# An attention and gated-MLP kernel: the second layer as seven half-size products, the first on 384 tokens at a time

## The chip, the cores and the metric

The kernel runs on one core of a Trainium2 chip. The metric is the time of one execution on the device, in microseconds (us). Three executions of the kernel before took 736.87, 735.04 and 735.07 us, a median of 735.07. One further execution was profiled; it took 735.57 us, of which its trace covers a span of 733.3 us. The core has five engines that work side by side: TensorE (PE in the profile; its weight loads are PEld) multiplies matrices into PSUM, VectorE (DVE) and ScalarE (ACT) work element by element, GpSimd (POOL) helps, and SP's queue issues nearly all transfers between the chip's memory and SBUF.

## The reference

Inputs are q, k, v of 4 batches x 8 heads x 768 positions x 64, and weights w_in (512 x 2,048) and w_out (2,048 x 512), the weights in float64.

```python
scores = scale * np.matmul(q, k.transpose(0, 1, 3, 2))
is_global = pos[None, :] < int(n_global)                 # n_global = 8
is_local = (rel >= 0) & (rel < int(n_local))             # n_local = 96
bias = -slopes[:, None, None] * dist[None, :, :]
scores = np.where(is_global | is_local, scores + bias, -1000000000.0)
a = softmax(scores)
x = (a @ v) as 3072 tokens x 512
h = x @ w_in
g = h * (1.0 / (1.0 + np.exp(-h)))
out = g @ w_out                                          # 3072 x 512, float32
```

Each position looks at 8 global positions and at the 96 up to itself. The two products of the MLP are 3,072 x 512 x 2,048 and 3,072 x 2,048 x 512.

## The kernel before, in words

The 3,072 tokens are 24 blocks of 128 (`B * NJ`). Three kinds of work share the engines.

*Attention*, block by block and, in a block, in four units of two heads: scores on TensorE (L507, or L531 in the first six blocks), a biased minimum on VectorE (L546), the exponential on ScalarE (L554), a transpose of the weights (L579), a copy (L585) and the product with v (L599 or L613). At the block's end its result is split into a high and a low part in the reduced matmul type, `xh` on ScalarE (L644) and `xl` on VectorE (L647).

*Layer one* (`moe_h`, L762) takes the tokens in groups of NB = 2 blocks, GT = 256 tokens, 12 groups. For each of 16 chunks `f` of 128 hidden features it adds up in PSUM, over four pieces `c` of the 512 inputs, three terms: high x high, high x low and low x high; each is one matmul whose stationary side is the weight and whose moving side is 256 tokens wide. ScalarE's tanh (L768) and VectorE (L772) turn the sum into the gate, which is stored to a DRAM tile (`moe_put`, L777).

*Layer two* (`moe_o`, L796) comes after the last group. Per group and pair of chunks it loads the gates back (`moe_get`, L781), splits them into `gh` (ScalarE, L785) and `gl` (VectorE, L789), and per 128 tokens adds up over 16 chunks three terms again; the stationary side is the gate, the moving side 512 columns of w_out. The sum is halved on its way out (L806 on ScalarE, L808 on VectorE) and stored.

The float64 weights are turned into float32 by three integer instructions on VectorE (`conv1` to `conv3`, L367, L373, L379) and split into a high part (L388, ScalarE) and a low part (L392, VectorE): 16 pieces of w_in, then 16 of w_out. Every piece of both weights is loaded a second time for two checks of its exponents (`check`, L410). At the end a judge (L871 to L901) gathers these and other conditions into one flag; if it is not zero, a general path (`general`) computes everything again.

The order is written out ahead of time. `Plan` holds every operation with an engine, a cost, a rank, what it depends on and which buffers it uses; `plan.run` (L95) steps through modelled time, and on each engine takes the ready operation of lowest rank whose buffers are free. The engines then work through their lists in that order. Attention has ranks 0 to 96 (a unit's number), layer one 1,000 and up, layer two 10,000 and up; gates and evictions come before everything (`FIRST`), the checks last (1e6). From the second group on, a unit's scores also wait for a chunk of layer one of the group before (L862 to L866: `AHEAD`, `PF`), so that attention and layer one keep step. `CAP` says how many PSUM banks each kind of result may hold, `HU` at which unit the shares change. `O0` and `ON` set the ranks of the conversions of w_out, `CF` and `CN` the chunks that the second loads for the checks wait for.

## Time and profile before

| | |
|---|---|
| median of three runs | 735.07 us |
| profiled execution | 735.57 us |
| its span | 733.3 us |
| PE busy (matmuls) | 721.6 us, 98% |
| PEld (weight loads) | 649.0 us, 89% |
| DVE | 452.2 us, 62% |
| ACT | 398.1 us, 54% |
| POOL | 28.9 us, 4% |
| moved by DMA | 114.34 MB, 155 GB/s over the span |

A matmul's busy time reaches from its start to the end of its way through the array, so that two neighbours overlap; how fast the engine takes them is read from start to start. The same holds, to a smaller degree, for VectorE and ScalarE. A wait is put down to the instruction whose end came last before the waiting one began.

### The profile page before, as it was taken

To read this page: it belongs to the slowest core of one execution; us is meant where nothing else is said; L and a number is where in the kernel's file an instruction comes from. 1 tells how busy PE (TensorE), PEld (TensorE's weight loads), DVE (VectorE), ACT (ScalarE), POOL (GpSimd) and SP (SyncE) were. 2 spreads that over 40 slices of the span, in tenths; PEclk is the share of its full clock that TensorE was granted. 3 is DMA by queue.
4 is the path that set the end of the run, shared out by engine and by line. 5 is a ranking of instruction groups with operands and counts; after the bars stand their busy time and mean duration, and the time that the engine had idled before them with its cause. 6 is when DMAs were issued, how large, how long until landed. Compare 5 with 4: busy or idle time off the path is not lost.

```text
span 733.3 us, 14421 instructions
## 1 busy us (share of the span) xinstructions
PE 721.6 (98%) x5170; PEld 649.0 (89%) x5170; DVE 452.2 (62%) x1307; ACT 398.1 (54%) x1009; POOL 28.9 (4%) x81
## 2 busy tenths in 40 slices
...
PEclk9999999999999999999999999999999999999999
...
GB/s 212 229 209 249 246 214 202 154 165 120 115 113 122 101 114 119 115 115 132 115 98 86 65 73 132 163 229 171 170 176 201 231 211 145 186 174 230 200 102 33
DMA packets 158975, 114.34 MB, mean 156 GB/s; under 512 B 98352, under 2 KB 139568, under 8 KB 158896
## 3 DMA queue, kind: packets, MB, share of 16 engines
...
q8 instruction: 42, 0.69, 0.4%
...
q10 hardware_dynamic: 432, 0.13, 0.1%
HBM read 81.86 MB, written 31.46 MB: 155 GB/s over the span
## 4 chain that ended last, share of the span: by engine, by line
PE 82%; DVE 11%; DMA 2%; ACT 2%; issue 2%; SPq 0%; ACTq 0%
PE bank L796 37%; PE bank L762 30%; PE bank L599 4%; PE bank L579 4%; PE bank L507 4%; PE bank L447 2%; DVE pe L546 2%; DVE wf L373 1%; DVE wf L379 1%; DVE th L772 1%; DVE wf L367 1%; DMA kn<-in_k_dram 1%; DVE WIL L392 1%; PE bank L531 1%; ACT pe L554 1%
## 5 line engine op out<-in xcount | busy, mean ns | idle before, releaser
L796 PE MATMUL bank<-wo,gh 128*128 128x512 f32 x768 | 241.6, 396 | 0.0
L762 PE MATMUL bank<-xh,WIH 128*128 128x256 f32 x768 | 226.5, 295 | 0.0
L762 PE MATMUL bank<-xh,WIL 128*128 128x256 f32 x768 | 216.0, 281 | 0.0
L762 PE MATMUL bank<-xl,WIH 128*128 128x256 f32 x768 | 215.7, 281 | 0.0
L796 PEld LDWEIGHTS bank<-wo,gh 128*128 128x128 f32 x768 | 144.1, 188 | 34.7
L785 ACT CAST gh<-gx 128x512 fp32r<-128x512 f32 x96 | 59.6, 620 | 174.6 <-PE bank L796 170.4
L796 PE MATMUL bank<-wo,gl 128*128 128x512 f32 x384 | 151.9, 396 | 0.0
L762 PEld LDWEIGHTS bank<-xh,WIH 128*128 128x128 f32 x768 | 145.1, 189 | 4.7 <-issue 4.1
L789 DVE TENSOR_TENSOR gl<-gx,gh 128x512 fp32r<-128x512 f32 x96 | 66.5, 692 | 129.8 <-ACT gh L785 129.7
L762 PEld LDWEIGHTS bank<-xl,WIH 128*128 128x128 f32 x768 | 145.2, 189 | 0.0
L762 PEld LDWEIGHTS bank<-xh,WIL 128*128 128x128 f32 x768 | 144.7, 188 | 0.1
L554 ACT ACTIVATE pe<-pe,NM 128x232 f32<-128x232 f32 (+1 forms) x192 | 90.3, 471 | 33.9 <-DVE NM L546 30.0
L768 ACT ACTIVATE th<-bank 128x256 f32<-128x256 f32 x192 | 72.9, 380 | 50.5 <-PE bank L762 46.8
L772 DVE SCALAR_TENSOR_TENSOR th<-th,bank 128x256 f32<-128x256 f32 x192 | 80.1, 417 | 21.2 <-ACT th L768 19.8
L796 PEld LDWEIGHTS bank<-wo,gl 128*128 128x128 f32 x384 | 72.1, 188 | 17.5
L546 DVE CUSTOM_DVE_ANT_0 pe<-bank,B 128x232 f32<-128x232 f32 (+1 forms) x192 | 69.2, 376 | 21.3 <-PE bank L507 14.5
L585 ACT COPY pt<-bank 128x512 f32<-128x512 f32 (+1 forms) x96 | 52.2, 545 | 9.1 <-PE bank L579 7.4
L579 PE MATMUL bank<-ident,pe 128*128 128x128 f32 (+1 forms) x352 | 55.7, 276 | 0.7 <-DVE pe L570 0.5
L410 DVE TENSOR_REDUCE TOP<-c 128x1 f32<-128x512 int16 x64 | 42.1, 679 | 13.5 <-DMA c<-in_moe_w_in_dram 6.8
L561 DVE TENSOR_SCALAR rs<-sm 128x2 f32<-128x2 f32 x72 | 12.4, 173 | 51.7 <-ACT pe L554 51.2
L579 PEld LDWEIGHTS bank<-ident,pe 128*128 128x128 f32 (+1 forms) x352 | 40.4, 137 | 3.9 <-DVE pe L570 1.2
L570 DVE TENSOR_SCALAR pe<-pe,rs 128x232 f32<-128x232 f32 (+1 forms) x144 | 42.0, 331 | 1.3
(107 smaller groups left out, 779.7 us busy)
## 6 DMA issues: line engine op xcount, KB each, us to landing
...
```

The costliest lines, as they stand in the source:

```text
L410: nc.vector.tensor_reduce(TOP[:, i, n:n + 1], top, AX.X, (ALU.min, ALU.max)[i], apply_absolute_value=True)
L546: nc.vector.tensor_tensor_reduce(t["p", hp][:, a, :n], t["s", hp][a][:, :n], B1[:, h] if i % NJ else B0[:, h], -SC, 3.0e38, ALU.add, ALU.m ...
L554: nc.scalar.activation(x, x, AF.Exp, bias=NM[:, i * H + h:i * H + h + 1], scale=-1.0, accum_out=t["sum", hp][:, a:a + 1],)
L570: nc.vector.tensor_scalar(x, x, t["inv", hp][:, a:a + 1], None, ALU.mult)
L579: nc.tensor.transpose(ps[:n, c, a], pe[:, a, c0:c0 + n], ident)
L585: nc.scalar.copy(t["pt", hp][:, c], t["tp", hp][:, c])
L762: nc.tensor.matmul(ph, w[:, c, fs], x[:, c], start=not c and not n, stop=c == NCC - 1 and n == 2)
L768: nc.scalar.activation(th, mo["ph", g, f], AF.Tanh, scale=0.5)
L772: nc.vector.scalar_tensor_tensor(gf, gf, 1.0, mo["ph", g, f], ALU.add, ALU.mult)
L785: nc.scalar.copy(gh, mo["g", g, f])
L789: nc.vector.tensor_sub(gl, mo["g", g, f], mo["gh", g, f].bitcast(F32))
L796: nc.tensor.matmul(po, a[:, s], w_o(w, f), start=f == 0 and n == 0, stop=f == NFC - 1 and n == 2)
```

## The change

Layer one works on groups of three blocks (NB = 3, 384 tokens, 8 groups). The gate's DRAM tile is laid out by block, so a chunk's store writes three pieces of 512 bytes per partition.

Layer two works on pairs of blocks, 12 of them. A pair's gates are a 2 x 2 array of quarters (block t, half k of the 2,048 features), w_out a 2 x 2 array of quarters (half of the features, half of the 512 columns), and the product is formed by Strassen's scheme in Winograd's form: seven products (`PROD`), each of a combination of the gate's quarters (`SUMS`: S1 to S4, four additions on VectorE per pair) with a combination of the weight's (`COMBINE`, four subtractions once per pair of row chunks). Each product adds up 8 chunks x 3 terms of 128 x 256 in one PSUM bank; seven evictions (`keep_half`, `add_half`, `add_kept`) add the products into the output tile. Each product's gate side is split once into high and low parts of 1,024 elements (`split_hi`, `split_lo`), into one of three pairs of buffers.

The weight w_out is converted in 8 pairs of row chunks; each pair has one float32 buffer `F` (seven blocks of 256) and two result tiles. Pairs 0 to 2 use the staging tiles of w_in. Pairs 3 to 6 lie in a pool `late`, opened when the attention's pools are closed (`open_late`, after the last block's `x_low`), pair 7 in the buffers of `xh` and `xl`. Loads from pair 4 on wait for chunk 6 of the last group but one. The tiles of w_in (`wi0` to `wi15`) are used again in layer two for quarters, splits and outputs.

The judge gets new conditions on scales: the largest |v| per block and partition within a factor of four of one of them (`scale_of`), and the largest entries of w_out by row and by column close to one of them (`top_size`, `col_turn`, `spread`). The checks of w_in move into the time of layer one, those of w_out stay in layer two. Other edits: `big` goes from 3 to 2 buffers and `R` gets a pool of its own; the gate's buffers go from six of 256 columns to four of 384; the attention units of the last group no longer wait for chunks of layer one.

```diff
-    CAP=dict(po=4, av=2, s=4, h=3, tp=2, tq=4), HU=9,
...
-    C0=8, CR=1, LW=12, LB=5, QB=3.5, RI=0.1, RN=0, RP=0.2, RM=0, RV=1.2, RQ=0.1, RB=3, LK=-25, LAG=1,
...
-    BP=(4, 3), CF=12, AHEAD=5, CN=5, I0=6, IV=6, QS='ACT', O0=2, ON=5, GA=6, PF=16,
+    CAP=dict(po=6, av=2, s=4, h=3, tp=2, tq=4), HU=13,
...
+    BP=(4, 3), CF=8, AHEAD=5, CN=19, I0=6, IV=6, QS='ACT', O0=14, ON=16, PF=16,
...
-    NB = 2
+    NB = 3
...
-        big=3, qkn=3, vn=2, vp=2, KH=2, KL=2, QH=2, QL=2, pe=3, pt=5, xh=2, xl=2, g1=6,
+        big=2, R=2, qkn=3, vn=2, vp=2, KH=2, KL=2, QH=2, QL=2, pe=3, pt=5, xh=2, xl=2, g1=4, F=1, gq=8, hl=3, ob=2,
...
     def stage(n, nm):
         if nm == "w" and n < NFC:
-            x = const.tile([P, 512, 2], U32, name=f"ws_{n}", tag=f"wo{HF + n % HF}")
+            t = const.tile([P, 3 * 512], U32, name=f"ws_{n}", tag=f"z{n % 7}")
+            st["f", n] = t[:, 1024:]
+            x = t[:, :1024].rearrange("p (f w) -> p f w", w=2)
         else:
-            x = sb3.tile([P, 512, 2], U32, name=f"{nm}_{n}", tag="big")
+            x = sbx.tile([P, 512, 2], U32, name=f"{nm}_{n}", tag="big")
         st[nm, n] = x
         nc.sync.dma_start(x if n >= NFC else x.rearrange("p (c f) w -> p c f w", c=NCC), source(n))
...
     def conv1(n):
-        if n < NFC:
-            f = const.tile([P, 512], U32, name=f"wf_{n}", tag=f"wo{n % HF}")
-        else:
-            f = sb2.tile([P, 512], U32, name=f"wf_{n}", tag="mid", bufs=5)
-        st["f", n] = f
+        if n >= NFC:
+            o, p = divmod(n - NFC, HF)
+            if not o:
+                st["F", p] = const.tile([P, 7, HM], F32, name=f"wq_{p}", tag="z6")
+            st["f", n] = st["F", p][:, 2 * o:2 * o + 2].rearrange("p a c -> p (a c)").bitcast(U32)
         nc.vector.tensor_scalar(
-            f, st["w", n][..., 1], 0x07FFFFFF, 3, ALU.bitwise_and, ALU.logical_shift_left
+            st["f", n], st["w", n][..., 1], 0x07FFFFFF, 3, ALU.bitwise_and, ALU.logical_shift_left
         )
...
+    COMBINE = ((5, 3, 1), (1, 1, 0), (4, 3, 1), (6, 2, 4))
+
+    def combine(p, i):
+        F = st["F", p]
+        x, a, b = COMBINE[i]
+        nc.vector.tensor_sub(F[:, x], F[:, a], F[:, b])
+
+    def pair_hi(p):
+        if p < 3:
+            x = [const.tile([P, 7, HM], F32R, name=f"wo_{p}_{i}", tag=f"z{2 * p + i}") for i in range(2)]
+        elif p < HF - 1:
+            x = [st["late"].tile([P, 7, HM], F32R, name=f"wo_{p}_{i}") for i in range(2)]
+        else:
+            x = [sbx.tile([P, 6, HM], F32R, name=f"wo_{p}_{i}", tag=("xh", "xl")[i]) for i in range(2)]
+            y = st["late"].tile([P, 2, HM], F32R, name="wo_last")
+            w2[p, 0, 6], w2[p, 1, 6] = y[:, 0], y[:, 1]
...
+        nc.scalar.copy(x[0], st["F", p][:, :n])
+        if n < 7:
+            nc.scalar.copy(w2[p, 0, 6], st["F", p][:, 6])
+
+    def pair_lo(p):
+        x = st["wo", p]
+        n = x[0].shape[1]
+        nc.vector.tensor_sub(x[1], st["F", p][:, :n], x[0].bitcast(F32))
+        if n < 7:
+            nc.vector.tensor_sub(w2[p, 1, 6], st["F", p][:, 6], w2[p, 0, 6].bitcast(F32))
...
+    def open_late():
+        attn.close()
+        st["late"] = ctx.enter_context(tc.tile_pool(name="late", bufs=1))
+
+    o_late = op("LATE", 0, 0, open_late)
+    o_w2, o_w2d = [], []
+    for p in range(HF):
+        rank = 4 * PAR["O0"] + PAR["ON"] * p
+        F, ops = Buf("F"), []
+        for n in (NFC + p, NFC + HF + p):
+            a = Buf("big")
+            o = op("DMA", 1456, rank - PAR["LW"], (lambda n=n: stage(n, "w")), [o_w[-1][1]], [a], PAR["DL"])
+            o_w2d.append(o)
+            o = op("DVE", 335, rank, (lambda n=n: conv1(n)), [o, *ops], [a, F])
+            o = op("DVE", 602, rank, (lambda n=n: conv2(n)), [o], [a, F])
+            o = op("DVE", 602, rank, (lambda n=n: conv3(n)), [o], [a, F])
+            ops = [o]
+        for i in range(4):
+            o = op("DVE", 335, rank, (lambda p=p, i=i: combine(p, i)), [o], [F])
+        a = []
+        if p == HF - 1:
+            a = [Buf("xh"), Buf("xl")]
+            for x in a:
+                x.left = 1
+        hi = op("ACT", ACT(7 * HM), rank, (lambda p=p: pair_hi(p)), [o] + ([o_late] if p > 2 else []), [F, *a])
+        lo = op("DVE", DVE(7 * HM), rank, (lambda p=p: pair_lo(p)), [hi], [F, *a])
+        o_w2.append((hi, lo))
+
...
+    def top_size(n):
+        nc.vector.tensor_reduce(
+            WM[:, n - NFC:n - NFC + 1], size_of(n), AX.X, ALU.max, apply_absolute_value=True
+        )
...
+        if n >= NFC:
+            o_vm.append(op("DVE", 602, 1e6 + n, (lambda n=n: top_size(n)), [o], [a]))
...
+    def scale_of(i):
+        nc.vector.tensor_reduce(
+            VM[:, i:i + 1], blk[i]["v"].rearrange("p h d -> p (h d)"), AX.X, ALU.max, apply_absolute_value=True
+        )
...
-                last = op("PE", ((1860 if j else 980) if stacked else 726 if j else 508), u - PAR["RV"],
+                last = op("PE", ((2100 if j else 1250) if stacked else 726 if j else 508), u - PAR["RV"],
...
-        for n, (w, x) in enumerate(((WIH, xh), (WIH, xl), (WIL, xh))):
+        for n, (w, x) in enumerate(((0, xh), (0, xl), (1, xh))):
             nc.tensor.matmul(
-                ph, w[:, c, fs], x[:, c], start=not c and not n, stop=c == NCC - 1 and n == 2
+                ph, w1[f][:, w, c], x[:, c], start=not c and not n, stop=c == NCC - 1 and n == 2
             )
...
-            gate[g] = dram.tile([P, NFC, GT], F32, name=f"gate{g}")
-        nc.sync.dma_start(gate[g][:, f], mo["th", g, f])
...
+            gate[g] = dram.tile([P, NB, NFC, P], F32, name=f"gate{g}")
+        nc.sync.dma_start(gate[g][:, :, f], mo["th", g, f].rearrange("p (b t) -> p b t", b=NB))
...
+    PART, HL, OUT = ((0, 3, 6, 7), (12, 13, 14, 15)), ((1, 2), (4, 5), (8, 9)), (10, 11)
+
+    def quarter(g, n):
+        t, k = divmod(n, 2)
+        b, j = divmod(2 * g + t, NB)
+        mo["a", g, n] = x = const.tile([P, HF, P], F32, name=f"a_{g}_{n}", tag=f"wi{PART[g % 2][n]}")
+        nc.sync.dma_start(x, gate[b][:, j, k * HF:(k + 1) * HF])
...
+    SUMS = dict(S1=(2, 3), S2=("S1", 0), S3=(0, 2), S4=(1, "S2"))
+
+    def sums(g, n):
+        if not st.get("S"):
+            st["S"] = [sbx.tile([P, HF, P], F32, name=f"S{i}", tag=("xh", "xl")[i]) for i in range(2)]
+        mo["a", g, n] = x = st["S"][int(n[1]) % 2]
+        a, b = (mo["a", g, y] for y in SUMS[n])
+        nc.vector.tensor_tensor(x, a, b, ALU.add if n == "S1" else ALU.subtract)
+
+
+
+    PROD = ((0, 0), (1, 2), ("S2", 4), ("S1", 1), ("S3", 5), ("S4", 3), (3, 6))
+
+    def split_hi(g, m):
+        r = HL[(7 * g + m) % len(HL)]
+        x = [const.tile([P, HF, P], F32R, name=f"g{i}_{g}_{m}", tag=f"wi{r[i]}") for i in range(2)]
+        mo["hl", g, m] = x
+        nc.scalar.copy(x[0], mo["a", g, PROD[m][0]])
+
+    def split_lo(g, m):
+        x = mo["hl", g, m]
+        nc.vector.tensor_sub(x[1], mo["a", g, PROD[m][0]], x[0].bitcast(F32))
+
+    def product(g, m, p, po):
+        mo["po", g, m] = y = bank(po, HM)
+        a, c = mo["hl", g, m], PROD[m][1]
+        for n, (i, w) in enumerate(((0, 0), (0, 1), (1, 0))):
             nc.tensor.matmul(
-                po, a[:, s], w_o(w, f), start=f == 0 and n == 0, stop=f == NFC - 1 and n == 2
+                y, a[i][:, p], w2[p, w, c], start=not p and not n, stop=p == HF - 1 and n == 2,
             )
...
+    def keep_half(g, m):
+        if m:
+            st["E", g] = sbx.tile([P, HM], F32, name=f"E_{g}", tag="th", bufs=4)
+        nc.scalar.mul(st["E", g] if m else place(g, 0), mo["po", g, m], 0.5)
+
+    def add_half(g, m, n, x):
+        nc.vector.scalar_tensor_tensor(place(g, n), mo["po", g, m], 0.5, place(g, x), ALU.mult, ALU.add)
+
+    def add_kept(g):
+        place(g, 0)
+        x = mo["out", g].rearrange("p a c n -> p (a c) n")
+        nc.vector.tensor_add(x[:, 1::2], x[:, 1:3], st["E", g].unsqueeze(1).to_broadcast([P, 2, HM]))
...
-                o = op("PE", 355, rank, (lambda g=g, f=f, c=c, h=ph: moe_h(g, f, c, h)),
+                o = op("PE", 528, rank, (lambda g=g, f=f, c=c, h=ph: moe_h(g, f, c, h)),
                        [o, *o_w[f]] + o_x[g], [ph, xb[g]["xh"], xb[g]["xl"]])
                 if f == c == g == 0:
...
+            t = op("ACT", ACT(GT), FIRST + rank, (lambda g=g, f=f: moe_tanh(g, f)), [o], [ph, th])
+            t = op("DVE", DVE(GT), FIRST + rank, (lambda g=g, f=f: moe_gate(g, f)), [t], [ph, th])
+            o_put[g, f] = op("DMA", 546, FIRST + rank, (lambda g=g, f=f: moe_put(g, f)), [t], [th], PAR["DO"])
...
+                o = op("PE", 355, r, (lambda g=g, m=m, p=p, po=po: product(g, m, p, po)),
+                       [hi, lo, *o_w2[p], o], [hl, po])
+                if not g and not m and not p:
+                    o["hold"] = 2
+            o_p.append(o)
+            e = FIRST + r
+            if m in (0, 3):
+                ev[m] = op("ACT", ACT(HM), e, (lambda g=g, m=m: keep_half(g, m)),
+                           [o] + (was(*OUT) if not g else []), [po, E if m else ob])
+            elif m == 1:
+                o_1, po_1 = o, po
+            else:
+                n, x = {2: (1, 0), 4: (2, 1), 5: (1, 1), 6: (2, 2)}[m]
+                ev[m] = op("DVE", 335, e, (lambda g=g, m=m, n=n, x=x: add_half(g, m, n, x)), [o, *ev.values()], [po, ob])
+                if m == 2:
+                    ev[1] = op("DVE", 335, e, (lambda g=g: add_half(g, 1, 0, 0)), [o_1, ev[2]], [po_1, ob])
+                elif m == 4:
+                    ev[7] = op("DVE", 602, e, (lambda g=g: add_kept(g)), [ev[4], ev[3]], [E, ob])
+                else:
+                    op("DMA", 728, e, (lambda g=g, t=m - 5: moe_out(g, t)), [ev[m], ev[1]], [ob], PAR["DO"])
...
+    plan.after(o_late, *(o for x in o_x for o in x))
+    for o in o_w2d[8:]:
+        plan.after(o, o_h[NGRP - 2, 6])
...
-        if f >= PAR["PF"]:
+        if f >= PAR["PF"] and g < NGRP - 1:
...
+    def spread(tp):
+        st["rvp"] = ps = bank(tp)[:, :2]
+        nc.tensor.matmul(ps, ident[:, 0:1].to_broadcast([P, P]), RV[:, 0:2], start=True, stop=True)
...
     for n, o in enumerate(o_cd):
-        plan.after(o, o_o[PAR["CF"] + PAR["CN"] * n])
-    o = steps(judge, [70, 270, 100, 70, 270, 100, 70, 270, 100, 70, 70, 70, 70], -1, o_c + o_x[-1], ())
+        if n < NFC:
+            plan.after(o, o_h[divmod(2 * NFC + 4 * n, NFC)])
+        else:
+            plan.after(o, o_p[2 + 5 * (n - NFC) - 3 * (n > NFC)])
...
+    o = op("PE", 440, 1e4 + 14, (lambda tp=tq: col_turn(tp)), [o_cd[NFC]], [cbuf[NFC], tq])
+    o = op("DVE", 602, 1e6, col_max, [o], [tq])
+    o = op("DVE", 140, 1e6, first_of, [o, *o_vm])
+    o = op("PE", 220, 1e4 + 15, (lambda tp=tr: spread(tp)), [o], [tr])
+    o = op("DVE", 70, 1e6, spread_move, [o], [tr])
+    o = steps(judge, [70, 70, 70, 70, 100, 70, 70, 70, 270, 100, 70, 270, 100, 70, 270, 100, 70, 70, 70, 70, 70, 70], -1, [*o_c, *o_x[-1], o], ())
...
```

## Rows read from the trace of the kernel before

**Rows 1.** The page's first part: busy us of each engine, its share of the span and its instructions; and from the second part the granted TensorE clock in 40 slices (9 is 90% of full speed or more).

```profile
PE 721.6 (98%) x5170; PEld 649.0 (89%) x5170; DVE 452.2 (62%) x1307; ACT 398.1 (54%) x1009; POOL 28.9 (4%) x81
...
PEclk9999999999999999999999999999999999999999
```

**Rows 2.** The chain of work that ended last, in order of time: start us, us, what. Two transfers in the first 100 us, and the last three pieces.

```profile
70.39 7.07 DMA kn<-in_k_dram
...
86.48 5.03 DMA w<-in_moe_w_out_dram
...
431.96 26.11 PE bank L762 x219
458.07 245.00 PE bank L796 x1050
703.18 24.00 PE bank L796 x102
```

**Rows 3.** Busy us (and instructions) of every engine in stretches of the whole kernel, with their length, the granted clock, the DMA engines' share and GB/s.

```profile
0.00:10.00 10.00, 7.41 (x33) 4.57 (x34) 3.95 (x22) 4.49 (x14) 3.10 (x13) 1.00 0.69 142
10.00:20.00 10.00, 10.00 (x63) 7.27 (x61) 4.63 (x24) 7.61 (x31) 0.66 (x2) 1.00 1.06 302
20.00:32.00 12.00, 12.00 (x111) 10.94 (x107) 11.90 (x29) 9.11 (x25) 1.26 (x2) 1.00 1.13 292
32.00:44.00 12.00, 11.95 (x101) 11.23 (x102) 11.97 (x38) 9.11 (x27) 0.21 (x1) 1.00 0.43 112
44.00:60.00 16.00, 16.00 (x139) 15.14 (x138) 15.86 (x43) 12.72 (x35) 0.72 (x2) 1.00 0.86 237
60.00:80.00 20.00, 17.91 (x147) 16.51 (x146) 19.79 (x48) 12.70 (x33) 2.57 (x1) 1.00 0.89 249
80.00:100.00 20.00, 19.81 (x161) 18.18 (x159) 15.18 (x40) 14.66 (x36) 0.00 (x0) 1.00 0.90 233
100.00:160.00 60.00, 59.39 (x517) 56.59 (x516) 57.36 (x177) 47.53 (x128) 5.20 (x14) 1.00 0.63 182
160.00:432.00 272.00, 271.96 (x2546) 266.42 (x2544) 187.87 (x688) 207.15 (x557) 15.12 (x48) 1.00 0.41 109
432.00:458.00 26.00, 26.00 (x220) 26.00 (x221) 9.15 (x21) 8.51 (x21) 0.00 (x0) 1.00 0.33 110
458.00:727.00 269.00, 269.00 (x1155) 216.16 (x1153) 113.87 (x186) 64.15 (x106) 0.00 (x0) 1.00 0.53 177
```

The columns between the length and the clock are PE, PEld, DVE, ACT and POOL.

**Rows 4.** VectorE's instructions in order of time, in a stretch where it is never idle: start us, us, line, operation, out<-in, sizes. What one costs is the step from its start to the next one's.

```profile
35.56 0.68 DVE L373 SCALAR_TENSOR_TENSOR wf<-ws,wf 128x512 uint32<-128x512 uint32 x1
36.28 0.69 DVE L379 SCALAR_TENSOR_TENSOR wf<-ws,wf 128x512 uint32<-128x512 uint32 x1
...
37.22 0.41 DVE L772 SCALAR_TENSOR_TENSOR th<-th,bank 128x256 f32<-128x256 f32 x1
37.55 0.69 DVE L373 SCALAR_TENSOR_TENSOR wf<-ws,wf 128x512 uint32<-128x512 uint32 x1
...
55.76 0.68 DVE L392 TENSOR_TENSOR wo<-wf,wo 128x512 fp32r<-128x512 f32 x1
56.36 0.68 DVE L392 TENSOR_TENSOR WIL<-wf,WIH 128x512 fp32r<-128x512 f32 x1
```

**Rows 5.** ScalarE's instructions in order of time in layer two, two that follow without a gap.

```profile
502.90 0.60 ACT L806 ACTIVATE osb<-bank 128x512 f32<-128x512 f32 x1 [2.41 <-PE bank L796]
503.40 0.61 ACT L785 CAST gh<-gx 128x512 fp32r<-128x512 f32 x1
```

**Rows 6.** Groups by line, engine, operation and size: busy us of the group, mean ns of one, idle us before them.

```profile
L762 PEld LDWEIGHTS bank<-xh,WIL 128*128 128x128 f32 x768 | 144.7, 188 | 0.1
...
L789 DVE TENSOR_TENSOR gl<-gx,gh 128x512 fp32r<-128x512 f32 x96 | 66.5, 692 | 129.8 <-ACT gh L785 129.7
...
L785 ACT CAST gh<-gx 128x512 fp32r<-128x512 f32 x96 | 59.6, 620 | 174.6 <-PE bank L796 170.4 <-DMA gx<-gate 4.2
L585 ACT COPY pt<-bank 128x512 f32<-128x512 f32 x80 | 46.4, 581 | 7.2 <-PE bank L579 5.6
...
L585 ACT COPY pt<-bank 128x256 f32<-128x256 f32 x16 | 5.8, 363 | 1.9 <-PE bank L579 1.8
```

**Rows 7.** The joint of the two layers in order of time: the first cast, subtraction and matmul of layer two.

```profile
456.56 0.62 ACT L785 CAST gh<-gx 128x512 fp32r<-128x512 f32 x1 [0.90 <-DMA gx<-gate]
...
457.21 0.69 DVE L789 TENSOR_TENSOR gl<-gx,gh 128x512 fp32r<-128x512 f32 x1 [1.10 <-ACT gh L785]
...
457.91 0.62 PE L796 MATMUL bank<-wo,gh 128*128 128x512 f32 x2
```

**Rows 8.** The low part of a block's attention result, in order of time on VectorE: those of the second and the third block, and the last of 24.

```profile
30.87 0.68 DVE L647 TENSOR_TENSOR xl<-bank,xh 128x512 fp32r<-128x512 f32 x1
...
43.85 0.68 DVE L647 TENSOR_TENSOR xl<-bank,xh 128x512 fp32r<-128x512 f32 x1
...
432.63 0.69 DVE L647 TENSOR_TENSOR xl<-bank,xh 128x512 fp32r<-128x512 f32 x1 [2.63 <-ACT xh L644]
```

**Rows 9.** Layer one's matmuls and weight loads alone (L762) in one stretch: length, PE busy (count), PEld busy (count), clock, DMA share, GB/s.

```profile
32.00:44.00 12.00, 5.54 (x37) 4.63 (x38) 1.00 0.43 112
```

**Rows 10.** Who waited for whom: us in total, times, longest us.

```profile
DVE TOP L410 <- DMA c<-in_moe_w_out_dram: 6.6, 4, 3.1
```

**Rows 11.** The last instructions of the span in order of time (SPq and ACTq are the issues of transfers).

```profile
726.78 0.40 PE L796 MATMUL bank<-wo,gl 128*128 128x512 f32 x1
727.21 0.38 ACT L806 ACTIVATE osb<-bank 128x256 f32<-128x256 f32 x1 [5.22 <-PE bank L796]
727.23 1.19 SPq L814 DMA_DIRECT2D out_dram<-osb  x2
727.62 0.36 ACTq L814 DMA_DIRECT2D out_dram<-osb  x1
727.63 0.43 DVE L808 TENSOR_SCALAR osb<-bank 128x256 f32<-128x256 f32 x1 [0.43 <-ACT osb L806]
```

More of the change, by code (lines that the diff above doesn't have):

```diff
@@ new lines, in pair_lo @@
+    def pair_lo(p):
+        x = st["wo", p]
+        n = x[0].shape[1]
+        nc.vector.tensor_sub(x[1], st["F", p][:, :n], x[0].bitcast(F32))
+        if n < 7:
+            nc.vector.tensor_sub(w2[p, 1, 6], st["F", p][:, 6], w2[p, 0, 6].bitcast(F32))
+    o_w = []
+    for n in range(NFC):
+        rank = PAR["C0"] + PAR["CR"] * n
+        o = op("DMA", 2000, rank - PAR["LW"], (lambda n=n: stage(n, "w")), [o_w[n - 7][1]] if n > 6 else (), (), PAR["DW"])
+        o = op("DVE", 335, rank, (lambda n=n: conv1(n)), [o])
+        o = op("DVE", 602, rank, (lambda n=n: conv2(n)), [o])
+        o = op("DVE", 602, rank, (lambda n=n: conv3(n)), [o])
+        hi = op("ACT", 520, rank, (lambda n=n: conv_hi(n)), [o])
+        lo = op("DVE", 602, rank, (lambda n=n: conv_lo(n)), [hi])
+        o_w.append((hi, lo))
@@ L647, in x_low @@
         nc.vector.tensor_sub(x_part(i, "xl"), blk[i]["av"], x_part(i, "xh").bitcast(F32))
[L649 removed]
+    kb = [{x: Buf(x) for x in ("KH", "KL", "QH", "QL", "vn", "vp")} | {"R": Buf("R")} for _ in range(B * NJ)]
     xb = [{x: Buf(x) for x in ("xh", "xl")} for _ in range(NGRP)]
@@ L796, in moe_o, with place @@
             nc.tensor.matmul(
[L797 removed]
+                y, a[i][:, p], w2[p, w, c], start=not p and not n, stop=p == HF - 1 and n == 2,
             )
[L800 removed]
+    def place(g, n):
         if ("out", g) not in mo:
[L802 to L808 removed]
```

208 lines of the change are left out of this document (107 added, 101 removed).

## The prediction, made before the change was run

> **What bounds the kernel now.** I read the engines' totals first [rows 1]: the matmul side of TensorE is busy for 721.6 of the 733.3 us span at the full granted clock, 2.4 GHz, while VectorE stands at 62% and ScalarE at 54%. Busy time of pipelined matmuls can hide gaps, so next comes the chain of work that ended last [rows 2]: its end is one run of first-layer matmuls and then nothing but second-layer matmuls, 269.0 us from 458.07 to 727.07. The table of stretches [rows 3] splits the rest. From 32 us on TensorE is full except in 60 to 100 us; from 20 to 80 us VectorE is full as well; from 458 us on VectorE is busy 114 of 269 us. So three stages: a start in which TensorE waits, a long one in which attention and layer one share a full TensorE, and layer two, TensorE alone. A change in the count or width of matmuls should show in full, provided that the other engines can still feed it.
>
> **Layer two.** Before: 24 blocks of 128 tokens x 16 chunks x 3 terms = 1,152 matmuls of 512 columns; 269.0 / 1,152 = 233.5 ns each [rows 2]. After: 12 pairs x 7 products x 8 chunks x 3 terms = 2,016 matmuls of 256 columns. That width is layer one's of today, each with its own weight load; alone on the engine 219 of them took 26.11 us, 119.2 ns each [rows 2]. (A missing record or two would make it 118.) 2,016 x 0.1192 = 240.3 us, so **-28.7 us**. One eighth of the columns would be -33.6; narrower matmuls give back 5.
>
> **Layer one.** Before: 12 groups x 16 x 4 x 3 = 2,304 matmuls, 274.6 us at 119.2 ns. After: 1,536 of 384 columns. No row has that width. From below by three quarters of a 512-column matmul, 175.1 ns; from above by one and a half of the 256-column one, 178.8; the straight line between the two gives 176.4, which I take: 270.9 us, **-3.7 us** (bounds -5.7 and 0).
>
> A rule of the Trainium skill speaks against narrow matmuls: TensorE: Matmul & The Clock Gate, Back-to-back issue gap, gives a stream of load and matmul about 81 ns at 128 columns and 131 at 512. By a straight line, an estimate, 256 columns would take 98 ns, and layer two would go from 151 to 197 us, 46 slower instead of 29 faster. The trace disagrees: 119.2 against 233.5 ns, nearly in proportion to the columns.
>
> **What has to feed layer two.** VectorE's instructions overlap at their ends, so I price them from start to start [rows 4]: 512 elements 0.60 us, 256 elements 0.33, one that reads what the last wrote 0.72. Along that line 1,024 elements are 0.60 + 2 x 0.27 = 1.14. Per pair: 7 lower halves and 4 sums, 11 x 1.14 = 12.5; 5 half-blocks out of PSUM x 0.33 and one of 512 columns, 2.3; the checks of w_out that stay here, 16 x 3 x 0.60 / 12 = 2.4. Together **17.2 us of VectorE against 168 x 0.1192 = 20.0 us of TensorE**, 86%. ScalarE: 512 elements cost 0.50 us from start to start [rows 5]; on the slope of its copies of 256 and 512 elements (0.22 us per 256 [rows 6]) 7 x 0.94 + 2 x 0.28 = 7.1 us per pair. So TensorE stays the bound if work is prepared ahead: a cast and a subtraction of 1,024 elements end about 2.3 us after they begin (0.62 + 0.44 and 0.69 + 0.54 [rows 6]; today's cast, subtraction and matmul hand over within 0.05 us [rows 7]), and three buffers allow two products, 5.7 us. I price this at 0; it can't be less, since TensorE's full pace is already counted, and its upper bound is a rival. The loads are 2 MB per pair as today, the outputs the same bytes. The first four wait on SP's queue for chunks of layer one's last group; behind them stand that group's gate stores, whose buffers the gates, and behind these PSUM and TensorE, need back. The four chunks awaited are spread over the group, as today's first loads are, so 0; a store held back for all four buffers would cost some 2 us a chunk.
>
> **The handover between the layers.** The new weights are 7 combinations of 4 blocks for each of 8 row pairs; per pair on VectorE 2 x (0.33 + 0.60 + 0.60) + 4 x 0.33 + a 1,792-element subtraction (0.60 + 5 x 0.27 = 1.95) = 6.3 us, and 1.6 us on ScalarE. Pairs 0 to 2 are made during attention. Pairs 3 to 7 can be written only when the attention's pools are closed, and 4 to 7 aren't loaded before chunk 6 of the group before the last. They go one after the other through one buffer: about 6.3 + 1.6 + ten dependent steps x 0.12 + gates that fall between = 10 us each, 40 for four. From that chunk to the end of layer one lie 25 chunks x 12 x 0.176 = 53 us, less some 5 for the load: 8 us to spare, if attention is over by then. Today it ends at 432.6 [rows 8], 25 us before layer two, because its units are held back chunk by chunk; the last group's are now let go, so it should end early in the last group but one. At the joint itself, S1 and S2 can only be formed after layer one's last matmul: 1.23 + 1.23 + 1.06 + 1.23 and a gate of 0.5 are 5.25 us against 5.7 of two products already prepared. **+0.5 us** (0 to 15).
>
> **The start.** Layer one now begins when three blocks are ready, not two. The third is finished at 43.9 us [rows 8], and 37 layer-one matmuls ran in 32 to 44 us [rows 9]: 4.4 us of filling is lost if nothing takes its place. Against it, the conversion of w_out (34 us of VectorE, 8 MB of DMA) leaves the first 160 us. VectorE, full from 20 to 80, gets room, and the two transfer waits in the chain, 7.07 us for k and 5.03 for w_out [rows 2], lose a cause; TensorE stood still for only 2.3 us around them [rows 3]. New there: a maximum over v per block, 0.60 us of VectorE each, and the checks of w_in, which fill what w_out leaves. **+4.4 - 2.3 = +2.1 us** (-6, all excess of 40 to 160 us gone, to +8).
>
> **The rest.** Five small matmuls for the judge, 0.7 us on the path. One of them (`spread`) waits on TensorE for the last check of w_out, with the last products queued behind it; checks wait up to 3.1 us for their loads today [rows 10], so 0 to 3.1 more. I take 0, since today's flag matmul waits for VectorE in the same place. The judge's 22 small instructions stand before the last products and VectorE has 14% room: 0 (4 us if they all stood in the way, at 0.2 each). The end: today ScalarE then VectorE move the last block, 0.85 us, and two queues store it [rows 11]; after, one VectorE instruction and one store of twice the size: 0 (-0.4 to +1). The 384-token gate is stored in 512-byte pieces instead of 1 KB; the queues have slack in that stage (DMA share 0.41 in 160 to 432 us [rows 3]): 0. If that cover is gone, four gate buffers of 2.1 us each hold as much time as six of 1.4 do now.
>
> Sum, on the profiled execution (735.57 us, span 733.3): -28.7 - 3.7 + 0.5 + 2.1 + 0.7 = -29.1, so 706.5. The median of the runs is 0.5 lower, so **706**.
>
> **Rivals.** (a) *The weights come late at the handover.* For it: a chain of 10 us steps with 8 us in hand, and a rank below every gate. Against it: the attention's last group is let go. If attention ends only with the last group but one, 3.5 + 40 us stand against 34 us of the last group: +10, at worst +20: 711 to 726.
> (b) *The start loses more.* Conversions of w_in keep VectorE full [rows 3], and with three blocks to finish first nothing fills TensorE: +5 to +12 beyond my +2, 711 to 718.
> (c) *Slower: preparation sets the pace of layer two.* If the in-order queues of ScalarE and VectorE let a product's cast, subtraction, sums and evictions run only one after the other, one product costs 1.06 + 1.23 + 4/7 x 1.23 + 0.32 + 0.34 = 3.65 us against 24 x 0.1192 = 2.86; 84 x 0.79 = +66, about 772. It decides from 2.86 us per product on, and makes the kernel slower than today from 3.2. For it: eleven long VectorE instructions per pair, two of them in a chain (S1, S2). Against it: the two engines overlap today, and VectorE alone needs 2.46 per product. In between, at 3.2, all is given back and the time is as before.
> (d) *Slower: weight loads aren't hidden.* By their recorded 188 ns [rows 6] 2,016 loads would be 379 us, +139 on 240: 845. The 219 pairs at 119.2 ns speak against it. By the Trainium skill's page named above it would be 781.
> (e) *The change does not do what it says*: the judge's new conditions send the run to the general path. The time would be some multiple; nothing in the trace speaks for it.
>
> **How the numbers follow.** My forecast 0.72, with 701 to 711 as its own range; (a) 0.12; (b) 0.07; (c) 0.06, of which 0.02 near no change; (d) 0.02; (e) 0.01. The forecast and a start or handover that goes better reach down to 699; up to 720 it takes in (b) and over half of (a); outside lie about 0.17. A measurement of this kernel tells about 0.3% from no change, 2.2 us. Faster: forecast, (a) and (b), 0.91. Same: 0.02. Slower: 0.07.
>
> **What would show it.** Right: layer-two matmuls start 119 ns apart and layer one's 176; the last run of the chain is TensorE alone for about 240 us; the stretch from the last layer-one matmul to the first of layer two has no gap over 1 us; VectorE is near 85% in that stage, with waits of its own for ScalarE. Wrong: idle time of TensorE behind the subtraction or the sums in layer two (c), behind the weights' lower halves at the joint (a), or a first layer-one matmul later than 45 us with idle time after it (b). A layer two above 250 us or a joint of over 10 us makes the prediction wrong; so would a start that gains more than 6.

## The result, and the profile after

710.75 us, median of 4 runs (709.95 to 712.21), beside 735.97 for the kernel before on the same chip: ratio 0.9656, 95% interval [0.9628, 0.9684]. Forecast: 706, range 699 to 720. The profiled execution took 710.94 us, its span 709.2.

The page's engine totals and clock, after, beside [rows 1]:

```profile
PE 694.5 (98%) x5294; PEld 664.6 (94%) x5294; DVE 590.5 (83%) x1416; ACT 425.1 (60%) x938; POOL 26.1 (4%) x81
...
PEclk9999999999999999999999999999999999999999
```

TensorE is still the bound; VectorE went from 452 to 591 us. Where the time went shows in the chain that ended last (start us, us, what):

```profile
113.18 5.17 DMA vn<-in_v_dram
...
156.62 5.01 DMA vn<-in_v_dram
...
401.16 62.21 PE bank L833 x351
463.37 42.69 PE bank L888 x360
...
698.30 5.17 PE bank L888 x42
```

Layer two (L888) runs from 463.37 to 703.47: 240.1 us for 269.0 [rows 2]. Layer one alone (L833) takes 62.21 / 351 = 177.2 ns per matmul. The joint has no gap. But all that stands ahead of layer two ends at 463.37, not at 458.07 [rows 2], though its own matmuls are cheaper. Two loads of v have entered the chain; [rows 2] had k and w_out in their place.

The stretches, with the columns of [rows 3]:

```profile
32.00:44.00 12.00, 11.73 (x100) 9.94 (x100) 11.87 (x34) 9.25 (x26) 0.72 (x2) 1.00 1.11 268
60.00:80.00 20.00, 20.00 (x147) 17.93 (x147) 19.37 (x54) 15.75 (x41) 1.32 (x4) 1.00 1.07 226
80.00:100.00 20.00, 19.05 (x131) 17.43 (x130) 15.97 (x53) 19.52 (x53) 1.26 (x4) 1.00 0.82 197
100.00:130.00 30.00, 28.11 (x173) 27.25 (x172) 26.44 (x68) 16.15 (x37) 1.26 (x4) 0.94 0.52 155
...
118.00:121.00 3.00, 1.11 (x8) 0.68 (x7) 2.63 (x11) 2.08 (x5) 0.00 (x0) 1.00 0.36 114
121.00:125.00 4.00, 4.00 (x17) 4.00 (x16) 4.00 (x9) 1.39 (x4) 0.00 (x0) 0.57 0.26 83
125.00:130.00 5.00, 5.00 (x36) 5.00 (x36) 4.31 (x19) 3.79 (x12) 1.26 (x4) 1.00 0.54 166
350.00:380.00 30.00, 28.35 (x230) 26.30 (x227) 26.63 (x100) 26.80 (x69) 2.69 (x8) 1.00 0.45 116
543.00:583.00 40.00, 40.00 (x340) 40.00 (x339) 35.03 (x43) 15.71 (x18) 0.00 (x0) 1.00 0.52 172
```

In layer two (543 to 583) TensorE has no gap beside a VectorE at 88%. At 118 to 121 it does 1.11 of 3 us, and in the 4 us after that it is busy throughout but gets through 17 matmuls, at a granted clock of 0.57: mostly the lower level, 1.2 GHz. The timeline says who made it wait (idle before an instruction, and its releaser, in brackets), and shows the joint:

```profile
112.00 0.55 DVE L843 SCALAR_TENSOR_TENSOR th<-th,bank 128x384 f32<-128x384 f32 x1
...
112.57 0.51 SPq L848 DMA_DIRECT2D gate<-th  x1
...
113.18 0.57 SPq L498 DMA_DIRECT2D vn<-in_v_dram  x1
...
118.37 0.69 DVE L511 TENSOR_REDUCE VM<-vn 128x1 f32<-128x512 f32 x1 [1.21 <-DMA vn<-in_v_dram]
...
119.04 0.55 DVE L843 SCALAR_TENSOR_TENSOR th<-th,bank 128x384 f32<-128x384 f32 x1
...
119.88 0.59 DVE L641 TENSOR_SCALAR pe<-pe,rs 128x232 f32<-128x232 f32 x2
...
120.28 0.32 PE L650 MATMUL bank<-ident,pe 128*104 128x128 f32 x1 [1.89 <-DVE pe L641]
...
434.43 2.03 DVE L419 TENSOR_TENSOR wo<-wq,wo 128x1792 fp32r<-128x1792 f32 x1 [1.29 <-ACT wo L412]
...
449.24 2.02 DVE L419 TENSOR_TENSOR wo<-wq,wo 128x1792 fp32r<-128x1792 f32 x1 [1.76 <-ACT wo L412]
...
459.72 1.76 DVE L419 TENSOR_TENSOR wo<-wq,wo 128x1536 fp32r<-128x1536 f32 x1 [0.62 <-ACT wo L412]
...
463.03 0.34 PE L833 MATMUL bank<-xh,wi 128*128 128x384 f32 x1
463.21 0.51 PE L888 MATMUL bank<-wo,g 128*128 128x256 f32 x3
463.23 1.23 DVE L868 TENSOR_TENSOR S<-a,a 128x1024 f32<-128x1024 f32 x1 [0.49 <-PE bank L833]
```

L511 is the judge's maximum over v (`scale_of`), new in this kernel. SP's queue issues v's load (113.18) just behind a gate store that could start only when VectorE's gate was done (112.57). The load lands 5.2 us later. VectorE stands at L511 until then, though a gate (L843) and, soon behind it, the normalisation of the softmax (L641) come next in its queue. TensorE needs that normalisation for its transposes and stops for 1.89 us. The same happens once more at 161.66 us, where TensorE loses 1.26. Of the 24 maxima six wait for their load, up to 1.4 us each. The group of this instruction (busy us, mean ns, idle before it):

```profile
L511 DVE TENSOR_REDUCE VM<-vn 128x1 f32<-128x512 f32 x24 | 16.3, 681 | 5.7 <-DMA vn<-in_v_dram 5.6
```

### The profile page after: what moved, and what is told of

The parts are those of the page before. It is cut to its first block, busy times and chain, and to the rows that moved or that the text cites. A ratio compares the mean times of both kernels' runs of the same rounds, so it can differ in the third digit from the quotient of the medians.

```text
span 709.2 us, 14385 instructions
## 1 busy us (share of the span) xinstructions
PE 694.5 (98%) x5294; PEld 664.6 (94%) x5294; DVE 590.5 (83%) x1416; ACT 425.1 (60%) x938; POOL 26.1 (4%) x81
## 4 chain that ended last, share of the span: by engine, by line
PE 83%; DVE 9%; ACT 5%; DMA 2%; issue 1%; SPq 0%; DVEq 0%
PE bank L888 34%; PE bank L833 32%; PE bank L650 4%; PE bank L670 4%; PE bank L578 3%; PE bank L518 2%; ACT pe L625 1%; DMA vn<-in_v_dram 1%; PE bank L684 1%; DVE pe L617 1%; PE bank L1103 1%; PE bank L602 1%; DVE th L843 1%; DVE ws L371 1%; DVE ws L377 1%
## 5 line engine op out<-in xcount | busy, mean ns | idle before, releaser
L833 PE MATMUL bank<-xh,wi 128*128 128x384 f32 x1024 | 293.3, 346 | 0.2 <-DVE KL L565 0.2
L888 PE MATMUL bank<-wo,g 128*128 128x256 f32 x1980 | 237.5, 281 | 0.0
L888 PEld LDWEIGHTS bank<-wo,g 128*128 128x128 f32 x1980 | 235.9, 189 | 0.0
L833 PEld LDWEIGHTS bank<-xh,wi 128*128 128x128 f32 x1024 | 188.7, 189 | 3.3 <-issue 2.5
L833 PE MATMUL bank<-xl,wi 128*128 128x384 f32 x512 | 173.1, 338 | 0.0
L833 PEld LDWEIGHTS bank<-xl,wi 128*128 128x128 f32 x512 | 97.1, 190 | 0.0
L839 ACT ACTIVATE th<-bank 128x384 f32<-128x384 f32 x128 | 62.1, 487 | 50.9 <-PE bank L833 50.2
L878 ACT CAST g<-S 128x1024 fp32r<-128x1024 f32 x48 | 49.9, 1049 | 61.0 <-DVE S L868 36.3
L843 DVE SCALAR_TENSOR_TENSOR th<-th,bank 128x384 f32<-128x384 f32 x128 | 69.8, 548 | 12.0 <-ACT th L839 11.5
L882 DVE TENSOR_TENSOR g<-S,g 128x1024 fp32r<-128x1024 f32 x48 | 58.4, 1220 | 15.0 <-ACT g L878 14.9
L878 ACT CAST g<-a 128x1024 fp32r<-128x1024 f32 x36 | 37.8, 1050 | 37.2 <-PE bank L888 35.2
L882 DVE TENSOR_TENSOR g<-a,g 128x1024 fp32r<-128x1024 f32 x36 | 43.9, 1219 | 3.3 <-ACT g L878 3.2
L641 DVE TENSOR_SCALAR pe<-pe,rs 128x232 f32<-128x232 f32 (+1 forms) x144 | 41.7, 331 | 1.2
```

What stands on the lines that cost most here:

```text
L641: nc.vector.tensor_scalar(x, x, t["inv", hp][:, a:a + 1], None, ALU.mult)
L833: nc.tensor.matmul(ph, w1[f][:, w, c], x[:, c], start=not c and not n, stop=c == NCC - 1 and n == 2)
L839: nc.scalar.activation(th, mo["ph", g, f], AF.Tanh, scale=0.5)
L843: nc.vector.scalar_tensor_tensor(gf, gf, 1.0, mo["ph", g, f], ALU.add, ALU.mult)
L878: nc.scalar.copy(x[0], mo["a", g, PROD[m][0]])
L882: nc.vector.tensor_sub(x[1], mo["a", g, PROD[m][0]], x[0].bitcast(F32))
```

## The experiments

Each is the changed kernel with one edit, unless the text says otherwise.

**vm_late: the maximum over v behind the use of v.** Its place in VectorE's order moves from ahead of the block's work to behind it; the work stays. `Plan` lays out the order anew around it, so other instructions change places too.

```
-        o_vm.append(op("DVE", 602, NHP * i + 2, (lambda i=i: scale_of(i)), list(o_v), [kk["vn"]]))
...
+        o_vm.append(op("DVE", 602, NHP * i + 4, (lambda i=i: scale_of(i)), [last], [kk["vn"]]))
```

> The maximum over v of a block (24 instructions on VectorE) is placed behind the block's product with v on TensorE, so that VectorE never stands waiting for the load of v; the work is the same. Theory A (the 4.8 us that the change took over the forecast come mainly from VectorE waiting in its queue for v, near 118 and 161 us, with the normalisation and TensorE's transposes behind it, and from the half clock that followed): 704 to 707 us, no wait of VectorE for v left, no granted clock under 0.95 in 100 to 160 us. Theory B (it is the 14 us of added VectorE work): 710 to 711, unchanged. Theory C (it is the attention of the last group, let go, that starves TensorE at 355 to 375 us): 710 to 711.

Measured: 707.58 us (705.74 to 708.40), ratio 0.9612 [0.9593, 0.9631]; span 704.0. First the same group, then the stretch, then the chain of this kernel:

```profile
L511 DVE TENSOR_REDUCE VM<-vn 128x1 f32<-128x512 f32 x24 | 16.3, 680 | 0.0
```

```profile
100.00:130.00 30.00, 29.89 (x196) 28.89 (x195) 26.81 (x73) 18.95 (x45) 1.72 (x4) 1.00 0.58 159
```

```profile
...
458.14 42.70 PE bank L888 x360
```

The same 24 instructions cost as much and no longer wait. TensorE gets 196 matmuls done in 100 to 130 us instead of 173, its clock stays full, and layer two starts 5.2 us earlier. Every run of this kernel is below every run of the changed one. By the ratios the change of place was worth 0.0044 x 736 = 3.2 us (the two intervals just touch), by the two profiles 5.2; the profiled run here is the fastest of five, so 5.2 is the upper figure. The time lies 0.6 us above theory A's range and 2.4 below that of B and C; its two signs, no wait for v and a full clock, came.

**vm_out: no maximum over v at all.** The 24 instructions are left out, and the judge sees a constant in their place.

```
+    nc.vector.memset(VM, 1.0)
...
-        o_vm.append(op("DVE", 602, NHP * i + 2, (lambda i=i: scale_of(i)), list(o_v), [kk["vn"]]))
```

> The maxima over v are left out (their results are set to 1, so the judge does not look at the scale of v). Theory A: within 1.5 us of the run that only places them later. Theory B: 3 us or more below that run. Theory C: 710 to 711.

Measured: 704.48 us (704.06 to 706.89), ratio 0.9579 [0.9559, 0.9599]; span 702.4. The chain:

```profile
...
456.61 42.70 PE bank L888 x360
```

0.0033 x 736 = 2.4 us below vm_late by the ratios (again intervals that touch), 1.6 by the profiles. By the medians it is 3.1. Theory A wanted at most 1.5, theory B at least 3: the result falls between. Of the 5.7 us (ratios; 6.8 by the profiles) that the maxima cost, the place is about half or more. The rest goes with the 14 us of work that they put on VectorE (24 x 0.60); how it splits is not shown.

**paced: attention's last group held back again.** Its units wait for layer one chunk by chunk, as those of the other groups do. This tests whether letting them go is what makes the handover work.

```
-        if f >= PAR["PF"] and g < NGRP - 1:
+        if f >= PAR["PF"]:
```

> The attention's last group is again held back by chunks of layer one. Theory C: the idle time of TensorE at 355 to 375 us goes, 706 to 708 us. The prediction's rival (a), a chain of 10 us per weight pair that then starts some 20 us later: the joint between the layers opens by 5 to 12 us, 714 to 722 us.

Measured: 719.62 us (718.87 to 723.93), ratio 0.9787 [0.9764, 0.9811]; span 717.1. Two stretches, and TensorE's order at the joint:

```profile
350.00:380.00 30.00, 30.00 (x238) 29.06 (x235) 23.61 (x81) 22.30 (x57) 2.53 (x8) 1.00 0.53 141
455.00:485.00 30.00, 23.41 (x143) 22.01 (x142) 25.38 (x35) 10.52 (x13) 0.00 (x0) 0.83 0.57 198
```

```profile
459.27 5.14 PE L888 MATMUL bank<-wo,g 128*128 128x256 f32 x42
466.32 0.50 PE L888 MATMUL bank<-wo,g 128*128 128x256 f32 x2 [1.91 <-ACT g L878]
468.04 3.88 PE L888 MATMUL bank<-wo,g 128*128 128x256 f32 x19 [1.22 <-DVE g L882]
472.59 0.39 PE L888 MATMUL bank<-wo,g 128*128 128x256 f32 x1 [0.67 <-ACT wo L412]
474.38 1.21 PE L888 MATMUL bank<-wo,g 128*128 128x256 f32 x8 [1.41 <-DVE wo L419]
```

This is rival (a), and more than it: TensorE loses 6.6 us around the joint, 2.1 of them on the two halves of the last weight pair (L412, L419), the other 4.5 on the splits of the gates (L878, L882), which share ScalarE and VectorE with that pair's conversion. The clock of the stretch falls to 0.83. The 1.65 us that TensorE stands still at 350 to 380 with the group let go do disappear, and layer two begins 3.9 us sooner (459.27 for 463.21); the joint takes more than that back. The balance is 0.0131 x 736 = 9.6 us worse.

**nb2: groups of 256 tokens again**, with what belongs to that size: six gate buffers, layer one's cost in the plan, the unit at which the PSUM shares change (`HU` 9 for 13) and the chunk that the later weight loads wait for. The core of the edit:

```
-    NB = 3
+    NB = 2
...
-        plan.after(o, o_h[NGRP - 2, 6])
+        plan.after(o, o_h[NGRP - 3, 9])
```

> Layer one again on groups of 256 tokens (12 groups, six gate buffers of 256), layer two as changed; the loads of the later weight pairs wait for a chunk of the last group but two. By the terms of the prediction: layer one's own matmuls cost 2.4 to 3.7 us more, the start is 4.4 us shorter, so 708 to 711 us with the first layer-one matmul near 32 us instead of 44. If 384 tokens matter for something else (fewer switches between kinds of matmul), 714 us or more.

Measured: 725.69 us (723.48 to 728.47), ratio 0.9866 [0.9841, 0.9892]; span 723.2. That is far above the 708 to 711 of the prediction's terms; the other branch, 714 or more, gave a reason (fewer switches) that the trace does not bear out. Two lines of TensorE's order, the chain, and L833 alone in the stretch of [rows 9]:

```profile
463.53 1.24 PE L888 MATMUL bank<-wo,g 128*128 128x256 f32 x9
...
476.69 0.79 PE L888 MATMUL bank<-wo,g 128*128 128x256 f32 x2 [5.18 <-ACT g L878]
```

```profile
464.75 7.49 DMA a<-gate
...
489.21 209.94 PE bank L888 x1768
...
712.30 5.17 PE bank L888 x42
```

```profile
32.00:44.00 12.00, 5.01 (x30) 3.94 (x30) 1.00 0.48 105
```

The start came back as expected (30 layer-one matmuls in 32 to 44 us; the changed kernel has 3, in 0.76 us). But layer two begins no sooner, at 463.53 for 463.21: what the start gave was lost before the joint, where TensorE stands still for 5.8 us between 160 and 280 us, against 1.4 between 160 and 350 in the changed kernel. And layer two takes 253.9 us from there to 717.47, for 240.1: that is 13.8 of the 14.0 us between the spans. A gate's load of 7.49 us stands in the chain, TensorE waits 5.18 us for the split behind it, and layer two runs without stops only from 489 us on. A last group of 23 us (16 x 12 x 0.119) leaves less time for the weights and the first gate loads than one of 34; that this is the reason is argued, not shown.

**eight: the same half-size products without the scheme.** Plain sums with 8 half-size products per pair, so no S1 to S4, no weight combinations. The core of the edit:

```
-    PROD = ((0, 0), (1, 2), ("S2", 4), ("S1", 1), ("S3", 5), ("S4", 3), (3, 6))
+    PROD = ((0, 0), (1, 1), (2, 0), (3, 1))
...
-                y, a[i][:, p], w2[p, w, c], start=not p and not n, stop=p == HF - 1 and n == 2,
+                y, a[i][:, p], w2[p, w, 2 * k + c], start=not k and not p and not n, stop=k == 1 and p == HF - 1 and n == 2,
```

> Layer two without the scheme, everything else as changed: each pair's four quarters are split as they are, and eight half-size products of 256 columns are added up in PSUM; no sums, no combinations of weights, four evictions per pair. 12 x 8 x 24 = 2,304 matmuls. If the term of layer two is right (119 ns each, TensorE alone), layer two takes 274 to 275 us, 34 more than as changed, and the kernel 743 to 746: slower than before, since 256 columns cost 5 to 6 us more than 512 for the same product. If preparation or weight loads had a share in layer two's pace, it takes less than 30 us more.

Measured: 745.62 us (744.92 to 746.38), ratio 1.0128 [1.0112, 1.0145]; span 743.2. The chain:

```profile
463.13 51.23 PE bank L878 x432
...
693.09 44.32 PE bank L878 x372
```

Layer two takes 274.3 us from 463.13 to 737.41 for 2,304 matmuls, again 119 ns each. Narrower matmuls alone cost 274.3 - 269.0 = 5.3 us, the seventh product for the eighth saves 274.3 - 240.1 = 34.2. Layer two begins at the same time (463.13 and 463.37): ahead of it no cost of the scheme shows.

**dve_x2 and dve_x3: how much VectorE has in hand.** The checks of w_out in layer two (3 instructions of 512 elements for each of 16 pieces) are done twice, then three times; the lines stand behind the first check of a piece.

```
+            for _ in range(1):
+                for i in range(2):
+                    o_c.append(op("DVE", 602, 1e6 + n, (lambda n=n, i=i: check(n, i)), [o], [a]))
+                o_vm.append(op("DVE", 602, 1e6 + n, (lambda n=n: top_size(n)), [o], [a]))
```

(dve_x3: `range(2)`.)

> As changed, but the three checks of each piece of w_out are done twice: 48 more instructions of 0.60 us on VectorE in layer two. By prices from start to start VectorE has 19.6 us of work per pair against TensorE's 20.0: layer two stays at 240 to 243 us, the kernel at 710 to 714. By recorded durations (1.22, 0.42, 0.68) it would have 21.6: layer two 258 to 260, the kernel 728 to 731, and rival (c) decides already.

> As changed, with the three checks of each piece of w_out done three times: 22.0 us of VectorE per pair from start to start against 20.0 of TensorE. VectorE becomes the bound while checks last (75 of 84 products): layer two 260 to 266 us, the kernel 730 to 737. If TensorE still holds its pace, VectorE's price is lower than I have it.

Measured: dve_x2 713.38 us (713.24 to 716.93), ratio 0.9703 [0.9678, 0.9728]; dve_x3 741.91 us (740.16 to 743.35), ratio 1.0077 [1.0055, 1.0100]. Layer two in dve_x2:

```profile
543.00:583.00 40.00, 40.00 (x340) 40.00 (x339) 40.00 (x54) 15.62 (x18) 0.00 (x0) 1.00 0.53 172
```

And in dve_x3, two stretches, then who waited for whom (us, times, longest):

```profile
663.00:703.00 40.00, 40.00 (x339) 40.00 (x339) 40.00 (x56) 14.15 (x17) 0.00 (x0) 1.00 0.16 54
703.00:735.00 32.00, 2.97 (x23) 2.58 (x21) 29.43 (x71) 0.00 (x0) 0.00 (x0) 0.60 0.25 82
```

```profile
PE bank L1027 <- DVE RV L1023: 24.4, 1, 24.4
...
PE bank L1085 <- DVE ok L1079: 3.0, 1, 3.0
```

In dve_x2 VectorE's recorded time fills the stretch (40.00 of 40 us), and TensorE still loses nothing in it: what an instruction costs here is the step between starts, not its recorded time. By that price each further set of checks adds 16 x 3 x 0.60 / 12 = 2.4 us per pair to 17.2: 19.6 of TensorE's 20.0 in dve_x2, 22.0 in dve_x3, and 12 x 2.0 = 24 us too much there. But it is not the products that slow down: TensorE is full up to 703 us. The checks have the lowest rank and pile up, and in the end TensorE waits 24.4 us for `spread` (L1027), which needs the last of them, then 3.0 for the flag, at a clock of 0.60. These last two were not in the expectation of dve_x3, which came out above it. The time of dve_x2 agrees with that of the changed kernel within the intervals; of the 2.3 us that its span is longer, 0.9 lie ahead of layer two and 1.7 behind the last product, where the flag's matmul waits 1.0 us for VectorE.

**best_a: vm_late with a handover that starts earlier.** Attention's last group is held back, but with 6 chunks more lead, and the loads of the later weights start after chunk 3 instead of 6 of the group before the last.

```
-        plan.after(o, o_h[NGRP - 2, 6])
+        plan.after(o, o_h[NGRP - 2, 3])
...
-        if f >= PAR["PF"] and g < NGRP - 1:
+        f -= 6 * (g == NGRP - 1)
+        if f >= PAR["PF"]:
```

> The maxima over v behind the product with v, as in the run before; the attention's last group held back again, but by six chunks less than the other groups; the loads of the weight pairs 4 to 7 wait for chunk 3 instead of 6 of the last group but one. Theory C in its smaller form (the last group, let go, starves TensorE by about 3 us at 350 to 380): 702 to 705 us with no joint gap. If the chain of weights has no room left: a gap at the joint of 1 to 5 us takes it back, 706 to 710.

Measured: 704.07 us (703.80 to 704.79), ratio 0.9564 [0.9551, 0.9577]; span 702.0. The chain:

```profile
...
456.33 42.59 PE bank L888 x357
```

It beats both kernels: below the changed one by more than either interval is wide, below vm_late by 3.5 us by the medians (2.0 by the profiles, 1.8 of it ahead of layer two). Which of its two further edits gives that wasn't separated.

## Why the prediction was right, and where it was off

**Layer two (-28.7).** 240.1 us measured, 240.3 forecast, at 119.1 ns per matmul; eight shows the two halves of the term, -34.2 and +5.3, apart. The Trainium skill, TensorE: Matmul & The Clock Gate, Back-to-back issue gap, gives for a stream of loads and matmuls a smaller gain than their width (131 ns at 512 columns, 81 at 128); the 119.1 ns at 256 columns here and in eight, beside 233.5 at 512 before, disagree with these figures. (The forecast ends layer two before at 727.07; by [rows 2] it is 703.18 + 24.00 = 727.18. Nothing hangs on the 0.1 us.)

**Layer one (-3.7).** 177.24 ns per matmul for the forecast's 176.4: 1,536 x 0.84 ns = 1.3 us less gain, inside the bounds.

**Feeding layer two (0), rival (c).** No stop in 543 to 583. The 17.2 of 20.0 us per pair, 86%, stands beside 88% of recorded time. dve_x2 shows that start-to-start steps were the right price, dve_x3 that the margin is real but under twice 2.4 us per pair. The form that rival (c) took there was not the forecast's: no slower products but one long wait at the judge.

**Handover (+0.5), rival (a).** No gap at the joint: last matmul of layer one 463.03, first of layer two 463.21. But the last full weight copy's lower half ended at 459.72 + 1.76 = 461.48, 1.9 us before layer one's end at 463.37, where the forecast saw 8 us to spare. From one pair's lower half to the next it took 10 to 15 us (436.46, 451.26, 461.48), not 10. That the joint held nevertheless was partly luck: the term was right, the margin was not. Paced shows that the argument (the last group is let go) was what carried it.

**Start (+4.4 - 2.3).** Three layer-one matmuls ran before 44 us, 37 before the change [rows 9]. From 32 to 60 us 27 filler matmuls (L1103, products of zeros that the plan puts where it sees TensorE idle; none there in the kernel before) took 4.41 us of that room: TensorE looks full there, but not with layer one. So the loss of 4.4 came as forecast. The gain of 2.3 did not come where it was expected: 60 to 80 us filled up (20.00 for 17.91), 80 to 100 lost (19.05 for 19.81), where now ScalarE is full (19.52 of 20), and VectorE is still full until 80. Nor did all of w_out's conversion leave the first 160 us, as the forecast had it: three of its eight pairs are converted there, 27.1 us of VectorE from 80 to 160 us. VectorE stood at 26.4 of 30 us in 100 to 130, where a maximum made it wait. The tile `wq` (float32 w_out, written and read) alone, VectorE and ScalarE:

```profile
100.00:130.00 30.00, 15.64 (x24) 3.37 (x2) 0.94 0.52 155
130.00:160.00 30.00, 9.67 (x16) 1.70 (x1) 1.00 0.56 141
```

**The step that failed: the maximum over v as 0.60 us of VectorE each.** The price was right (0.68 us recorded, 0.60 from its start to the next one's at 118.37), the place was not looked at. The forecast listed it as work in the start, and for `spread` it named what is queued behind a wait, but not for these 24. Each stands in a queue that VectorE works through in order, and six of them wait there for a load; at 113.18 that load stands in SP's queue behind a store that waited for VectorE. vm_late, whose edit is only that place, gives back 3.2 (ratios) to 5.2 us (profiles).

The account, on the profiled execution (706.5 forecast, 710.9 measured, +4.4): ahead of layer two 463.4 for 456.5 (458.07 - 3.7 + 2.1), +6.9, of which vm_late gives back 5.2 and layer one's longer step explains 1.3; layer two, joint and judge -1.4 (240.1 measured for 240.3 + 0.5 + 0.7); after the last product and outside the span -1.0 (7.5 us for 8.5). These last two, smaller than forecast, hide 2.4 us of the miss ahead of layer two. TensorE also stands still for 0.95 us in 80 to 100 and 1.65 in 350 to 380, which no term had; vm_late keeps both (0.97 and 2.15), and what offsets them there wasn't separated. The 706 is off by 4.8 and was right in direction and range because the large term was right to 0.2 us.
